# Moving elementwise work between engines in a gated linear attention with a rational MLP: denominator sums, decay products and transposed copies

## The chip, the cores and the metric

One core of a Trainium2 chip. Its engines work side by side, each through its own program in order, and meet at semaphores: TensorE (PE in the profile; its weight loads are PEld), VectorE (DVE), ScalarE (ACT), GpSimd (POOL) and SyncE (SP, which here only issues DMAs). The metric is device time of one execution in microseconds (us); lower is better.

## The reference, cut to what matters

An attention with a per-channel forget gate, 4 batches, 8 heads, 768 steps, 48 channels per head, and behind it an MLP whose activation is a rational function, on 3072 tokens.

```python
f = 1.0 / (1.0 + np.exp(-f_logit))
for t in range(S):
    state = f[:, :, t, :, None] * state + np.einsum('bhd,bhe->bhde', k[:, :, t], v[:, :, t])
    y[:, :, t] = np.einsum('bhd,bhde->bhe', q[:, :, t], state)
...
h = x @ w_in                      # x: 3072 x 384, w_in: 384 x 2048
P = a[0] + a[1] * h + a[2] * h2 + a[3] * h3
Q = 1.0 + np.abs(b[0]) * np.abs(h) + np.abs(b[1]) * h2
out = (P / (Q + 1e-06)) @ w_out
```

The inputs and the output are float32; the kernel's products run in bf16.

## The kernel before, in words

The work is cut into 12 units of 256 tokens, numbered n: unit n holds chunk n // 4 of batch n % 4, both halves of 128 tokens and all 8 heads. Units of one batch pass a state on, so unit n needs the state that unit n - 4 left.

Each unit goes through some thirty named steps, one small function each. The attention part:

- `ld` (L182) loads f, k, q through SP and v through GpSimd's queue. `ef` (L260) and `ls` (L264) on ScalarE make log(1 + exp(-f)); `cs` (L269) sums it along the steps by a matmul with a triangular matrix; `A` (L280) is its exponential with the sign for q (x = 0) or k (x = 1).
- `xa` (L288, the multiplication is L291) multiplies q or k by that decay: 128 partitions x 768, float32 in, bf16 out to `qkp`. Unit 0 does this in two halves, the 11 other units whole, so there are 22 whole products and 4 halves.
- `T` (L300) turns q and k over on TensorE; `Te` (L310, L315) copies the result, 128 x 2048 bf16, from PSUM to SBUF.
- `sc` (L319) makes the scores, `mk` (L333, L337) masks them, `sv` (L382) and `st` (L417) carry the state on, `yb`, `yi` (L367, L360) make y. They use `vm` (L339, L344), two small copies of parts of v on GpSimd. `ye` (L403) brings y to SBUF.

The MLP part, in halves of 8 of 16 blocks of the hidden size (a half is 128 x 2048):

- `h` (L423) is x @ w_in for 4 blocks, `hy` (L440) its copy to bf16, `sq` (L444, L446) h squared, `ab` (L452, L454) |h|, as `z`. The coefficients are scaled beforehand so that the denominator needs only the plain sum z + h squared.
- That sum is made in one of three ways. `u` (L457, L462) adds on TensorE: for 4 blocks, two matmuls with the identity for h squared and two for z into the same PSUM tile, which `ln` (L470, L473) on ScalarE then reads, 128 x 1024 at a time. `zd` (L480, L482) adds with a DMA that accumulates into z, and `lz` (L484, L487) takes the logarithm of z, 128 x 2048 at a time. `zv` (L476) adds on VectorE, also ahead of `lz`; nothing calls it in the kernel before. In before, half 0 to 8 of every unit goes through `u`, half 8 to 16 through `zd`.
- `ex` (L490, L495) makes exp(-log), the reciprocal of the denominator. `p1` (L498, L500), `p2` (L503, L505) and `pm` (L512, L514) make the two parts of the numerator on VectorE, `ta` (L516, L518) adds them with an accumulating DMA from GpSimd's queue, and `gm` (L524, L527) multiplies by the reciprocal.
- `o` (L529, L535) is the product with w_out, `oe` (L538) its copy out of PSUM, `so` the store.

PSUM is four slots, each used by one tile at a time: the number behind @ in a step names its slot. The pools of SBUF tiles are small: three buffers for what `ld` fills, three for `hy` and `gall`, two for `h2` and `z`, one for most of the attention.

The order is written out by hand: `manual_schedule` (L146) lets nothing be reordered, and ORDER (L19) is a list of all steps, split at ";". Each step is issued in that order on its engine, so the list sets every engine's program and the order within each DMA queue; waits between engines follow from the tiles. A step reads `name unit arguments`: `xa 1 0` is unit 1's product for q, `h 0 12 16 @0` is unit 0's blocks 12 to 15 into slot 0, `Te 0 0 2` is a half of unit 0's heads.

Of the kernel before, what the change touches and what calls it, by code (L numbers as in the profile page):

```python
# [29 lines left out]
hy 1 4 8; xa 2 1; cs 3 @2; hy 1 0 4; ld 4 k; p2 0 0 16; T 2 @3; A 3 0; u 0 0 4 @1; pm 0 8 16; A 3 1  # L30
u 0 4 8 @0; ld 5 f; ln 0 0 4; pm 0 0 8; ta 0 8 16; h 1 8 12 @2; ln 0 4 8; Te 2; vm 2 0; vm 2 1; lz 0 8 16
ta 0 0 8; ld 4 q; sq 1 0 8; sc 2 0 @0; h 1 12 16 @3; wo 0 4; ef 4; xa 3 1; sv 2 0 @1; hy 1 8 12; mk 2 0
ae 2; hy 1 12 16; xa 3 0; ls 4; sc 2 1 @3; st 2 0; T 3 @2; ex 0 0 8; mk 2 1; vm 3 1; vm 3 0; yb 2 0 2 @0
sq 1 8 16; yb 2 2 4; yi 2 1; sv 2 1; ye 2 s; cs 4 @3; Te 3; h 2 0 4 @0; A 4 0; st 2 1; A 4 1; ab 1 0 8
# [563 lines left out]
```

## Time and profile before

| | us |
|---|---|
| runs shown, median (lowest to highest) | 239.4 (238.78 to 239.57) |
| profiled execution | 240.47 |
| its span, first to last instruction of the program | 238.8 |

| engine | busy us | share of the span | instructions |
|---|---|---|---|
| TensorE | 213.7 | 89% | 3113 |
| VectorE | 206.0 | 86% | 232 |
| ScalarE | 190.6 | 80% | 197 |
| GpSimd | 61.7 | 26% | 91 |

Busy time is the time in which an engine has an instruction at work; matmuls are pipelined and their ends are modelled, so TensorE's figure is not TensorE at its peak. The DMA queues moved 43.71 MB; the queue of GpSimd's own DMAs 24.38 MB of it. The granted TensorE clock was 0.996 on mean.

In a line of the groups stand: the kernel's line, engine, operation, tile written <- tiles read, shapes, number; then busy us and mean ns of one; then the idle time of the engine just before them and what ended it. In a line of the timeline: start, duration, engine, line, operation, and in square brackets the idle time before it. L numbers are lines of the kernel before.

### The profile page before, as it was taken

The page shows a single profiled execution, that of the slowest core. Times are in us where ns is not written, and L with a number is a line of the kernel's source. Part 1 is how long each engine was busy: PE and PEld are TensorE (multiplying, and loading weights), DVE is VectorE, ACT ScalarE, POOL GpSimd, SP SyncE. Part 2 cuts the span into 40 slices and gives each one's busy share as a digit, 9 for nine tenths or more (in the row PEclk, how much of TensorE's full clock was granted, in tenths as well). Part 3 has the DMA queues.
Part 4 walks back from the last instruction along what each step waited for, and adds up shares of the span by engine and source line. Part 5 has one row for each costly group of instructions (what it writes and reads, how often), then busy time and mean ns, then how long its engine had stood idle before and what let it go on. Part 6 is the DMA issues. An engine that isn't in the chain of part 4 may idle for free.

```text
span 238.8 us, 7065 instructions
## 1 busy us (share of the span) xinstructions
PE 213.7 (89%) x3113; PEld 148.6 (62%) x3128; DVE 206.0 (86%) x232; ACT 190.6 (80%) x197; POOL 61.7 (26%) x91
## 2 busy tenths in 40 slices
PE   0489988798999989799999999999999999999990
PEld 0357765576575658467668778556866877764550
DVE  5395799989989699879899999998999899999630
ACT  4451879979969859959989999997966996999951
POOL 5322044231222205142404133304003311323200
PEclk9999999999999999999999999999999999999998
DMA  7999999999799999999895998799907995499954
GB/s 118 249 191 194 223 222 211 238 222 168 137 178 182 240 218 243 226 216 217 198 188 104 224 232 163 136 227 271 185 7 108 191 204 114 88 176 199 176 118 125
DMA packets 62239, 43.71 MB, mean 183 GB/s; under 512 B 51329, under 2 KB 57217, under 8 KB 62209
## 3 DMA queue, kind: packets, MB, share of 16 engines
q0 software_dynamic: 20976, 24.38, 62.6%
q1 hardware_dynamic: 41088, 18.88, 33.2%
q8 instruction: 24, 0.39, 0.6%
q14 instruction: 7, 0.05, 0.1%
q10 hardware_dynamic: 144, 0.00, 0.0%
HBM read 25.17 MB, written 4.72 MB: 125 GB/s over the span
## 4 chain that ended last, share of the span: by engine, by line
PE 63%; ACT 10%; DMA 10%; issue 7%; DVE 4%; SPq 4%; ACTq 0%; DVEq 0%; POOLq 0%
PE hp L428 22%; PE op L535 18%; PE u L462 6%; PE y L351 5%; DMA qn<-in_q_dram 5%; DMA gall<-hy 4%; PE tp L307 4%; SPq L190 3%; PE sc L329 3%; ACT qi L495 2%; PE cs L277 2%; ACT lq L487 2%; PE sv L399 2%; ACT hy L442 2%; ACT lq L473 2%
## 5 line engine op out<-in xcount | busy, mean ns | idle before, releaser
L535 PE MATMUL op<-w_out_sb,gall 128*128 128x384 bf16 x384 | 69.4, 327 | 3.5 <-issue 1.8
L428 PE MATMUL hp<-xT,w_in_sb 128*128 128x256 bf16 x576 | 68.6, 273 | 1.1 <-ACT xT L407 0.9
L428 PEld LDWEIGHTS <-w_in_sb 128*128 128x128 bf16 x576 | 55.2, 98 | 11.4 <-issue 1.3
L442 ACT CAST hy<-hp 128x1024 bf16<-128x1024 f32 x48 | 47.8, 1016 | 10.7 <-PE hp L428 10.4
L535 PEld LDWEIGHTS <-gall 128*128 128x128 bf16 x384 | 35.7, 98 | 28.7 <-issue 3.4
L495 ACT ACTIVATE qi<-lq 128x2048 bf16<-128x2048 f32 x24 | 45.9, 1918 | 0.2
L518 POOL DMA_DIRECT2D gall<-hy x24 | 22.4, 962 | 71.5 <-DVE gall L514 19.7
L527 DVE TENSOR_TENSOR gall<-gall,qi 128x2048 bf16<-128x2048 bf16 x24 | 29.2, 1219 | 4.0 <-DMA gall<-hy 2.4
L337 DVE TENSOR_TENSOR scm<-sc,mask 128x1024 bf16<-128x1024 f32 x24 | 29.0, 1219 | 3.2 <-PE sc L329 3.0
L482 POOL DMA_DIRECT2D z<-h x12 | 12.8, 1070 | 70.4 <-DVE z L454 22.4
L446 DVE TENSOR_TENSOR h<-hy 128x2048 bf16<-128x2048 bf16 x24 | 29.1, 1218 | 1.2 <-ACT hy L442 1.2
L514 DVE TENSOR_TENSOR gall<-gall,h 128x2048 bf16<-128x2048 bf16 x24 | 28.9, 1217 | 0.0
L473 ACT ACTIVATE lq<-u 128x1024 f32<-128x1024 f32 x24 | 24.2, 1031 | 3.1 <-PE u L462 2.7
L286 ACT ACTIVATE A<-cs 128x768 f32<-128x768 f32 (+1 forms) x26 | 18.7, 767 | 5.9 <-PE cs L277 5.5
L487 ACT ACTIVATE lq<-z 128x2048 f32<-128x2048 bf16 x12 | 23.0, 1921 | 0.0
L315 DVE COPY qkT<-tp 128x2048 bf16<-128x2048 bf16 (+1 forms) x13 | 14.8, 1139 | 5.5 <-PE y L351 3.2
L407 ACT ACTIVATE xT<-y 128x768 bf16<-128x768 f32 x12 | 9.7, 812 | 9.6 <-PE y L351 9.6
L277 PE MATMUL cs<-lsp,Ui 128*128 128x384 bf16 (+1 forms) x39 | 11.0, 347 | 7.2 <-ACT lsp L267 7.2
L454 DVE TENSOR_SCALAR z<-hy 128x2048 uint16<-128x2048 uint16 x24 | 16.8, 711 | 0.0
L344 POOL COPY vmp<-vn 128x128 bf16<-128x128 bf16 x24 | 11.8, 572 | 19.3 <-DMA vn<-in_v_dram 19.3
L505 DVE TENSOR_SCALAR hy<-hy,a_sb 128x4096 bf16<-128x4096 bf16 x12 | 16.6, 1384 | 0.0
L307 PE MATMUL tp<-ident,qkp 128*128 128x128 bf16 x192 | 14.8, 235 | 2.0 <-DVE qkp L291 1.9
(63 smaller groups left out, 269.4 us busy)
## 6 DMA issues: line engine op xcount, KB each, us to landing
gall<-hy POOLq DMA_DIRECT2D x24, 512.0 KB, 7.2
z<-h POOLq DMA_DIRECT2D x12, 512.0 KB, 6.1
out_dram<-osb SPq DMA_DIRECT2D x24, 192.0 KB, 3.9
fn<-in_f_logit_dram SPq DMA_DIRECT2D x11, 384.0 KB, 10.2
kn<-in_k_dram SPq DMA_DIRECT2D x11, 384.0 KB, 7.5
qn<-in_q_dram SPq DMA_DIRECT2D x11, 384.0 KB, 9.4
vn<-in_v_dram POOLq DMA_DIRECT2D x12, 192.0 KB, 8.8
w_out_sb<-in_moe_w_out_dram POOLq DMA_DIRECT2D x4, 384.0 KB, 9.7
```

The costliest lines, as they stand in the source:

```text
L307: nc.tensor.transpose(t[:, x, i, p, :], s["qk"][:, x, i, 2 * p:2 * p + 2, :].rearrange("t h d -> t (h d)"), ident)
L337: return nc.vector.tensor_mul(t, s["sc", g].rearrange("s r a i t -> s (r a) (i t)"), mb)
L428: nc.tensor.matmul(t[:, m - m0, :].rearrange("f (j t) -> f j t", j=UB), w_in_sb[:, kk, m * P:(m + 1) * P], s["x"][:, :, kk, :], start=(kk ...
L442: nc.scalar.copy(fl(big(s, "hy", "hy", 3), m0, m1), fl(s["hp", m0], 0, m1 - m0))
L446: return nc.vector.tensor_mul(fl(big(s, "h2", "h2", 2), m0, m1), fl(s["hy"], m0, m1), fl(s["hy"], m0, m1))
L473: nc.scalar.activation(fl(lq(s, g), m0 - 8 * g, m1 - 8 * g), fl(s["u", m0], 0, m1 - m0), AF.Ln, scale=regs[2], bias=1.0 + 1e-6)
L487: nc.scalar.activation(fl(lq(s, g), m0 - 8 * g, m1 - 8 * g), fl(s["z"], m0, m1), AF.Ln, scale=regs[2], bias=1.0 + 1e-6)
L495: nc.scalar.activation(fl(s["qi", g], m0 - 8 * g, m1 - 8 * g), fl(s["lq", g], m0 - 8 * g, m1 - 8 * g), AF.Exp, scale=-1.0)
L514: return nc.vector.tensor_mul(fl(s["g"], m0, m1), fl(s["g"], m0, m1), fl(s["h2"], m0, m1))
L518: nc.gpsimd.dma_start(out=fl(s["g"], m0, m1), in_=fl(s["hy"], m0, m1), accum_op=ALU.add)
L527: return nc.vector.tensor_mul(fl(s["g"], m0, m1), fl(s["g"], m0, m1), fl(s["qi", g], m0 - 8 * g, m1 - 8 * g))
L535: nc.tensor.matmul(s["op"][:, j, 0:DM], s["g"][:, m, C * j:C * j + C], w_out_sb[:, m, :], start=(s["on", j] == 1), stop=(s["on", j] == KF))
```

## The change

1. 20 of the 24 `u` steps with their 20 `ln` go (those of unit 1 and unit 11 stay). The 10 halves without them go through `zv` on VectorE or `zd` by DMA, and then `lz`. There are 12 `zd` before and after, of which 6 are the same halves; 6 others go from `zd` to `zv`, and 6 new ones come to `zd`. `zv` then does 10 halves: 0 (both), 2 (both), 1, 5, 6, 8 (8 to 16), 3, 4 (0 to 8).
2. 15 of the 22 whole products `xa` get a `p` and run on GpSimd, in its queue between DMA issues and `vm` copies.
3. `Te` of units 1, 2, 4, 10 and 11 get an `s` and run on ScalarE.
4. ORDER is another one throughout: 804 steps in place of 824. The loads at the start change places too.

The function `xa`, whose other form of the option goes:

```diff
-    def xa(n, x, a0=0, a1=HP, eng="v", mark=None):
+    def xa(n, x, *args):
         s = unit(n)
+        a0, a1 = [v for v in args if v != "p"] or (0, HP)
         hh = slice(2 * a0, 2 * a1)
-        i = (nc.gpsimd if eng == "p" else nc.vector).tensor_mul(
+        return (nc.gpsimd if "p" in args else nc.vector).tensor_mul(
             s["qk"][:, x, :, hh, 0:D],
             s["qk"[x]][:, hh].rearrange("p h i d -> p i h d"),
             s["A", x].rearrange("p i (h d) -> p i h d", h=H)[:, :, hh])
-        if mark is not None:
-            behind(i, mark)
-        return i
```

ORDER's start, before and after:

```diff
-cz 0; ab_ b a; ld 0 f 2 4; ld 0 v; ld 0 f 0 2; cz 3; cu 1; ld 0 k 0 2; cz 1; cu 0; ld 0 q 2 4; fa
-ld 0 q 0 2; ef 0 2 4; ld 0 k 2 4; cz 2; ef 0 0 2; ls 0 0 2; fr; ls 0 2 4; ci; cs 0 2 4 @1; vm 0 1
-ld 1 f; cs 0 0 2 @0; A 0 1 0 2; A 0 1 2 4; xa 0 1 0 2; A 0 0 2 4; vm 0 0; wi 8 16; ld 1 v; A 0 0 0 2; wi 4 8; xa 0 0 2 4
-ld 1 k; xa 0 0 0 2; xa 0 1 2 4; T 0 0 2 @2; T 0 2 4 @1; Te 0 0 2; Te 0 2 4; sc 0 0 @2; ld 1 q; sv 0 0 @0
...
-yb 0 0 2 @1; ld 2 f; yi 0 1; xa 1 0; yb 0 2 4; ld 2 q; wi 0 4; ye 0 s; fb; T 1 @3; st 0 1; h 0 12 16 @0
-Te 1; ld 3 f; sc 1 0 @2; hy 0 12 16; h 0 8 12 @1; mk 1 0; ef 2; vm 1 0; vm 1 1; sc 1 1 @3; ls 2; ld 2 v
...
+ci; ld 0 k 0 2; cu 0; ld 0 f 0 2; ab_ b a; ld 0 f 2 4; ld 0 v; cz 3; cz 1; cu 1; ld 0 q 2 4; ld 1 f; cz 2; ld 0 k 2 4
+cz 0; ld 0 q 0 2; ef 0 2 4; ld 1 k; fa; ld 1 q; ls 0 2 4; ef 0 0 2; ls 0 0 2; cs 0 2 4 @0; ld 2 f; cs 0 0 2 @3
+A 0 1 0 2; A 0 0 0 2; A 0 1 2 4; xa 0 1 0 2; ef 1; xa 0 1 2 4; ls 1; vm 0 1; wi 8 16; xa 0 0 0 2; cm; ab_ a s; ld 1 v
+sv 0 0 @2; A 0 0 2 4; wi 0 4; T 0 0 2 @3; cs 1 @1; xa 0 0 2 4; A 1 1; ae 0; Te 0 0 2; A 1 0; ld 3 f; T 0 2 4 @3
+xa 1 1; xa 1 0 p; sc 0 0 @1; Te 0 2 4; st 0 0; sc 0 1 @0; yi 0 1 @3; mk 0 0; vm 0 0; fr; mk 0 1; ef 2; T 1 @1; ld 2 q
+fb; yb 0 0 2; ls 2; Te 1 s; sv 0 1; wi 4 8; yb 0 2 4; st 0 1; sc 1 1 @0; ld 2 k; ld 3 q; mk 1 1; ye 0 s; ld 2 v
+cs 2 @1; sc 1 0 @3; A 2 1; A 2 0; ld 3 k; vm 1 0; mk 1 0; h 0 12 16 @2; ef 3; xa 2 0; h 0 8 12 @0; hy 0 12 16
+hy 0 8 12; sq 0 8 16; vm 1 1; sv 1 0 @3; h 0 0 4 @0; ld 3 v; ls 3; ld 4 f; ld 4 k; wo 8 12; ae 1; st 1 0; ab 0 8 16
```

A stretch of the middle, around unit 6's products, before (the lines of ORDER from `cs 6` on) and after:

```diff
-hy 4 12 16; ld 8 f; gm 2 0 8; ld 6 v; cs 6 @3; hy 4 0 4; pm 3 8 16; sc 5 0 @0; h 4 4 8 @1; ld 9 f; A 6 0
-mk 5 0; vm 5 0; vm 5 1; A 6 1; o 2 0 0 4 @2; ef 7; pm 3 0 8; sv 5 0 @3; hy 4 4 8; ld 7 k; o 2 1 0 4; xa 6 1
-o 2 0 4 8; ae 5; ls 7; st 5 0; yb 5 0 2 @0; ex 3 0 8; xa 6 0; yb 5 2 4; yi 5 1; o 2 1 12 16; p2 3 0 16
-T 6 @1; lz 3 8 16; ab 4 0 8; yi 5 0; ta 3 0 8; o 2 1 8 12; Te 6; sv 5 1; ta 3 8 16; o 2 1 4 8; ye 5 s
...
+o 1 1 0 4; cs 6 @2; zd 3 8 16; o 1 0 8 12; A 6 0; sv 4 1; gm 2 0 8; A 6 1; h 4 8 12 @0; so 0 0 2 s; oe 1 0 2 s
+h 4 12 16 @2; sc 5 1 @3; hy 4 8 12; hy 4 12 16; pm 3 8 16; so 1 0 2 s; st 4 1; h 4 4 8 @0; lz 3 0 8; mk 5 1; xa 6 0 p
+h 4 0 4 @2; o 2 1 4 8 @1; ld 9 f; hy 4 4 8; sv 5 0 @3; sq 4 8 16; ab 4 8 16; hy 4 0 4; o 2 0 0 4; ab 4 0 8; ls 7
+sq 4 0 8; o 2 0 12 16; zd 4 8 16; lz 3 8 16; ae 5; sc 5 0 @0; p2 3 0 16; ex 3 8 16; yi 5 0 @2; o 2 1 8 12; pm 3 0 8
+o 2 0 4 8; yb 5 2 4; ld 10 f; o 2 1 0 4; o 2 1 12 16; st 5 0; ex 3 0 8; mk 5 0; sv 5 1; yi 5 1; ta 3 8 16; st 5 1
+vm 6 1; xa 6 1 p; zv 4 0 8; ta 3 0 8; p1 4 0 16; yb 5 0 2; ld 7 v; cs 7 @0; ye 5 s; o 2 0 8 12; T 6 @3; A 7 0; ld 8 q
+sv 6 0 @2; A 7 1; Te 6; ef 8; h 5 4 8 @0; oe 2 0 2 s; ae 6; so 2 0 2 s; pm 4 8 16; hy 5 4 8; p2 4 0 16; xa 7 0 p
+ld 9 k; ls 8; h 5 0 4 @1; hy 5 0 4; sc 6 0 @3; cs 8 @0; mk 6 0; xa 7 1 p; st 6 0; ld 11 f; pm 4 0 8; gm 3 8 16
```

More of the change, by code (lines that the diff above doesn't have):

```diff
@@ L30 @@
[L30 to L34, printed above, removed]
@@ new lines @@
+p2 5 0 16; ye 7 s; pm 5 8 16; sv 7 1; ef 11; o 4 0 4 8; st 7 1; T 8 @1; ta 5 0 8; ta 5 8 16; ld 10 v; vm 9 0
+o 4 1 0 4; oe 4 0 2 s; zv 6 8 16; p1 6 0 16; h 7 12 16 @3; sv 8 0 @2; Te 8; cs 9 @0; so 4 0 2 s; hy 7 12 16; pm 6 0 8
+ae 8; vm 8 1; h 7 8 12 @3; lz 6 0 8; hy 7 8 12; h 7 0 4 @1; st 8 0; A 9 1; h 7 4 8 @2; p2 6 0 16; gm 5 0 8; ab 7 8 16
+A 9 0; hy 7 0 4; sq 7 8 16; o 5 1 0 4 @0; pm 6 8 16; sc 8 1 @1; hy 7 4 8; zd 7 8 16; xa 9 0; ta 6 0 8; gm 5 8 16
+mk 8 1; sc 8 0 @3; ls 10; o 5 0 0 4; o 5 1 4 8; cs 10 @2; o 5 0 12 16; ex 6 0 8; xa 9 1 p; lz 6 8 16; vm 8 0; A 10 0
@@ new lines @@
+sc 9 0 @2; sc 9 1 @0; yi 9 0 @1; sq 8 0 8; yi 9 1; o 6 0 8 12; mk 9 1; o 6 1 12 16; ex 7 0 8; o 6 0 12 16; o 6 1 8 12
+o 6 1 0 4; mk 9 0; ta 7 0 8; yb 9 0 2; oe 6 0 2 s; p1 8 0 16; yb 9 2 4; ab 8 0 8; zd 8 0 8; ye 9 s; T 10 @0; Te 10 s
+zv 8 8 16; h 9 4 8 @3; hy 9 4 8; h 9 0 4 @2; pm 8 0 8; sc 10 1 @3; so 6 0 2 s; p2 8 0 16; hy 9 0 4; ta 8 0 8
+lz 8 8 16; h 9 12 16 @0; pm 8 8 16; h 9 8 12 @1; gm 7 8 16; hy 9 12 16; sq 9 0 8; sv 10 0 @2; hy 9 8 12; ab 9 0 8
+o 7 1 8 12 @0; ex 8 8 16; gm 7 0 8; zd 9 0 8; sq 9 8 16; ab 9 8 16; o 7 0 8 12; sc 10 0 @1; o 7 0 4 8; o 7 1 4 8
@@ new lines @@
+o 7 1 0 4; vm 11 0; lz 8 0 8; o 7 1 12 16; o 7 0 12 16; ae 10; ex 8 0 8; mk 10 1; xa 11 0 p; o 7 0 0 4; mk 10 0
+zd 9 8 16; p1 9 0 16; T 11 @3; st 10 0; yi 10 0 @1; oe 7 0 2 s; vm 11 1; yi 10 1; vm 10 0; yb 10 0 2; yb 10 2 4
+p2 9 0 16; pm 9 8 16; Te 11 s; ye 10 s; gm 8 0 8; sv 11 0 @0; sc 11 0 @2; lz 9 0 8; h 10 4 8 @1; h 10 12 16 @3
+mk 11 0; ae 11; hy 10 4 8; st 11 0; h 10 8 12 @1; hy 10 12 16; pm 9 0 8; ta 8 8 16; ta 9 8 16; gm 8 8 16; sc 11 1 @0
+h 10 0 4 @2; hy 10 8 12; yb 11 0 2 @3; mk 11 1; yi 11 0; lz 9 8 16; ab 10 8 16; sq 10 8 16; ta 9 0 8; yb 11 2 4
@@ new lines @@
+pm 11 0 8; p2 11 0 16; u 11 0 4 @2; o 9 0 4 8; gm 10 8 16; ta 11 0 8; o 9 0 12 16; ln 11 4 8; ln 11 0 4; pm 11 8 16
+o 9 0 8 12; gm 10 0 8; o 10 0 8 12 @0; ta 11 8 16; o 10 1 12 16; lz 11 8 16; o 10 0 12 16; o 10 1 8 12; o 10 0 4 8
+o 10 0 0 4; o 10 1 0 4; ex 11 0 8; oe 8 0 2 s; o 10 1 4 8; gm 11 0 8; so 8 0 2 s; o 11 0 4 8 @2; ex 11 8 16
+o 11 1 4 8; o 11 0 0 4; o 11 1 0 4; oe 9 0 2 s; gm 11 8 16; oe 10 0 2 s; so 9 0 2 s; o 11 0 8 12; o 11 1 12 16
+so 10 0 2 s; o 11 1 8 12; o 11 0 12 16; oe 11 0 2 s; so 11 0 2 s
```

100 lines of the change are left out of this document (35 added, 65 removed).

## The prediction

> **What bounds the kernel now.** I read the page's busy times first, then a table of three stretches, then the groups by shape, then the timeline where GpSimd and VectorE meet.
>
> ```profile
> PE 213.7 (89%) x3113; PEld 148.6 (62%) x3128; DVE 206.0 (86%) x232; ACT 190.6 (80%) x197; POOL 61.7 (26%) x91
> ...
> PE   0489988798999989799999999999999999999990
> ...
> DVE  5395799989989699879899999998999899999630
> ```
>
> TensorE and VectorE are full in the same slices: neither alone is the bound. The table by stretch (time, busy PE, PEld, DVE, ACT, POOL) says how full.
>
> ```profile
> 0.00:30.00 30.00, 19.74 (x330) 14.20 (x331) 18.88 (x47) 14.49 (x22) 8.32 (x22) 1.00 1.11 195
> 30.00:220.00 190.00, 181.26 (x2711) 127.18 (x2724) 180.25 (x181) 164.93 (x167) 51.69 (x67) 1.00 0.97 185
> 220.00:238.80 18.80, 12.69 (x77) 7.19 (x75) 6.82 (x6) 11.13 (x9) 1.69 (x2) 0.95 0.65 142
> ```
>
> In the 190 us of the middle TensorE idles 8.7, VectorE 9.75, ScalarE 25.1. So taking work from TensorE gains only as much as VectorE can follow; VectorE decides the sum. The middle is where nearly all of the change lies.
>
> **The change, part by part.** The rows that price it, by shape (busy us, mean ns):
>
> ```profile
> L442 ACT CAST hy<-hp 128x1024 bf16<-128x1024 f32 x48 | 47.8, 1016 | 10.7 <-PE hp L428 10.4
> L446 DVE TENSOR_TENSOR h<-hy 128x2048 bf16<-128x2048 bf16 x24 | 29.1, 1218 | 1.2 <-ACT hy L442 1.2
> L473 ACT ACTIVATE lq<-u 128x1024 f32<-128x1024 f32 x24 | 24.2, 1031 | 3.1 <-PE u L462 2.7
> L487 ACT ACTIVATE lq<-z 128x2048 f32<-128x2048 bf16 x12 | 23.0, 1921 | 0.0
> L315 DVE COPY qkT<-tp 128x2048 bf16<-128x2048 bf16 x11 | 13.4, 1221 | 5.1 <-PE y L351 3.2 <-PE tp L307 1.8
> L291 DVE TENSOR_TENSOR qkp<-kn,A 128x768 bf16<-128x768 f32 x11 | 10.5, 951 | 2.1 <-DMA kn<-in_k_dram 1.8 <-ACT A L286 0.3
> ```
>
> TensorE: 20 of 24 u steps go, 4 matmuls each. The chain of work has four of them in 0.86 us at 144.75 us, so 20 × 0.86 = 17.2 us go. It had 8.7 idle in the middle; it will have some 25.
>
> VectorE, work alone: its instructions overlap by some 85 ns, so one costs its distance to the next in the timeline: 0.87 us for a product (L291), 1.13 for a 2048-column copy or tensor operation. 15 products go, -13.0; 5 transposed copies (L315) go, -5.65; 10 sums z + h (zv) come, priced as L446, which has the same shape and kinds, +11.3. Sum **-7.4**.
>
> ScalarE: 5 copies of 128x2048 from PSUM, which no row shows. L442 takes 1016 for 1024 columns and L407 812 for 768, 0.8 ns a column, so 1.83 us, 9.2 in all; 20 ln of 1.03 become 10 lz of 1.92, -1.4. Sum +7.8, covered by its 25.1 idle us in the middle; without that cover it would cost these 7.8. I take 0.
>
> DMAs: 12 accumulating zd remain 12 and 24 ta remain 24, of 512 KB each; the loads are the same. Only other halves go by DMA. Bytes cost 0; the new places of the loads are in the term for the start.
>
> GpSimd: 15 products of 128x768, two inputs. No row shows one. The nearest is L344, a copy of 128 columns with one input, 0.29 us when nothing is in its way. Six times its columns is 1.75 us; twice that, for two inputs, 3.5; VectorE's 0.95 is the lower end. I take 1.75, since the copy's time holds a fixed part that is not paid six times. The Trainium skill, GPSIMD Engine Reference, 3.1 Elementwise, gives about 2.6 cycles an element for two inputs at 1.2 GHz, an estimate of 1.7 us here; no run here shows it.
>
> What such a product does to VectorE is the dearest unknown. This is the timeline of both engines where copies meet them (start, duration, x2 is two merged):
>
> ```profile
> 105.14 2.35 DVE L446 TENSOR_TENSOR h<-hy 128x2048 bf16<-128x2048 bf16 x2
> 107.41 1.34 DVE L500 TENSOR_SCALAR gall<-hy,a_sb 128x4096 bf16<-128x4096 bf16 x1
> ```
> ```profile
> 107.21 1.67 POOL L344 COPY vmp<-vn 128x128 bf16<-128x128 bf16 x1
> ...
> 186.37 0.30 POOL L344 COPY vmp<-vn 128x128 bf16<-128x128 bf16 x1 [4.40 <-DMA vn<-in_v_dram]
> ```
>
> At 186.37 VectorE multiplies scores out of PSUM (L337) and the copy takes 0.30. At 107.21 VectorE works from SBUF: the copy began 0.28 before L446's end, was not done when L500 took over, and ended 0.13 us after L500. It took 1.67. The other way round is seen with a DMA's issue: L454, 0.69 as a rule, took 1.32 at 31.9, while GpSimd issued one from 31.4 on. So they hold each other up, unless VectorE reads PSUM (L337 29.0, L315 14.8, L419 11.0: 54.8 of 206 us, 27%; about a quarter after the change).
>
> Hence a product takes from VectorE between nothing (it falls beside PSUM work or idle time) and its whole 1.75 us: 0 to 26 for 15. If it meets VectorE at random, three quarters: 1.31. If VectorE's back-to-back instructions keep it out until a PSUM instruction of 1.13 comes, as at 107.2, 0.62. I take the mean, 0.96, so **+14.4**. This is more than the 0.87 that VectorE saved on it.
>
> VectorE's idle 9.75: the waits table puts 3.2 on y before L315, 3.0 on sc before L337, 2.3 on tp before L315, all TensorE, 8.5 in all. A freer TensorE can remove these (0 to -8.5). I take half, **-4.25**: the scores and states still come in a chain through ScalarE and VectorE itself.
>
> New waits: GpSimd's queue is in order, and behind each product stand ta and zd issues, loads of v and vm copies. In before gm (L527) waited 2.4 us in all for ta, so most have slack. The transposes are nearer: xa 6 1 on GpSimd, then T 6, then Te 6 on VectorE, with only zv 4 0 8 and p1 4 (2.4 us) between, against 1.75 + 1.0 of transposes + 0.6 to get in. One such microsecond, **+1** (0 to +5).
>
> Start: the load of q for unit 1 was the start's chain; it stays ninth on SP's queue, issued at 8.95, landed at 19.7. Its product now runs on GpSimd (+0.8) and Te 1 on ScalarE (+0.6), and h 0, at 22.04 in before, now stands behind sc 1 1, cs 2 and sc 1 0 on TensorE: about 26. But mk 1 and xa 2 0 are done by then, which before came later. Also on GpSimd, vm 0 0, w_in's third load and v for unit 2 wait behind that product; on SP, load 1 f (0.93 to issue) goes ahead of two halves of unit 0. I take **+2** (-1 to +4). End: the steps from h 11 on hold the same ScalarE work but one lz for two ln; 0.
>
> Sum: -7.4 + 14.4 - 4.25 + 1 + 2 = +5.75. The profiled execution took 240.47 (span 238.8 and 1.67 around it): 246.2. The median of the runs is 1.07 below it: **245.1 us**.
>
> **The rivals.**
> *Faster: the products fall beside PSUM work.* GpSimd has 177 idle us, TensorE is relieved, and all three engines could run near 198. Then a product takes 0.27 from VectorE (+4), the TensorE waits go wholly: -7.4 + 4 - 8.5 + 0 + 2 = -9.9, less 1.07: 229.5; with half of those waits 233.8; I put it at 232. It decides from 0.58 us a product down: (7.4 + 4.25 - 1 - 2) / 15. For it: at 180 to 187 us most copies met L315 or L337 and were not held. Against: a product is six times as long as a copy.
>
> *Whole exclusion.* The product holds VectorE's SBUF work for all its length whenever it has begun: 15 × 1.31 = 19.7 in place of 14.4, so +11: 250.4. The Trainium skill, SBUF — State Buffer, Who interferes with whom, speaks for it and against this change: a VectorE instruction with two SBUF inputs, or in a two-port mode, and a GpSimd instruction that reads SBUF lock each other out for the whole instruction. By that rule the 1.67 above is explained, and the trace agrees.
>
> *GpSimd's queue becomes the wait.* VectorE's runs keep products out for 2 to 3 us and the ta behind them reach gm late. Were every second product to pass 2.5 us on, 7 × 2.5 = 17: about 260. Against: gm's slack in before.
>
> **How the numbers follow.** Forecast 0.38 (own range 240.2 to 248, from 0.63 to 1.15 a product); faster 0.30; whole exclusion 0.17; queue 0.07; within 0.3% 0.08 (the terms cancel). This kernel's measurement can tell about 0.3% from no change, 238.7 to 240.1. So faster 0.30, same 0.08, slower 0.62. The range 231 to 257 takes in most of the faster case and whole exclusion with some queueing, and leaves out about 0.15.
>
> **What would show it.** Right: VectorE's busy time near 206 or above, with L291 down to 11 and L446, L514, L527, L454 longer than 1.22 and 0.69 on mean (or gaps before them with no releaser); GpSimd products of 1.75 to 4 us; TensorE near 196 with gaps before T and h. Wrong: those VectorE means unchanged, VectorE near 198 and TensorE's gaps small; then the faster case holds. If waits of L527 on ta lead the list, it is the queue. h 0 well before 26 us unmakes the start's term.

## The result, and the profile after

The changed kernel takes **248.68 us** (median of 4 runs, 247.75 to 249.15); the kernel before, run on the same chip, 239.09. The ratio is 1.0406, with a 95% interval of 1.0351 to 1.046. Forecast were 245.1 and the range 231 to 257: the sign and the range held, and the time lies 0.7 us above the forecast's own range. The profiled execution took 249.15 and its span 247.3, that is 8.5 more than before. Of a3, b2 and c1 below some executions were disturbed and took over 1.5% more than the fastest; the medians count these, the ratios leave them out, and the profiles of a3 and c1 are of such executions.

The page's busy times and slices (one digit for 6.2 us here) of the kernel after:

```profile
PE 206.3 (83%) x3045; PEld 146.0 (59%) x3048; DVE 208.6 (84%) x222; ACT 198.0 (80%) x192; POOL 103.9 (42%) x106
...
PE   0576987639958998999879999979979979799990
...
DVE  5373384999999989989999999999999995999630
...
PEclk9999999988995999999979999999999999999998
```

VectorE now leads, and its row is 9 from the eighth slice on almost without a break, while TensorE's has 7s among its 9s. Ahead of the eighth slice VectorE is emptier than before. Three stretches (time, busy PE, PEld, DVE, ACT, POOL, granted clock, DMA share, GB/s):

```profile
0.00:60.00 60.00, 38.90 (x637) 28.37 (x638) 38.91 (x67) 37.29 (x44) 24.59 (x35) 0.97 1.12 210
60.00:220.00 160.00, 146.90 (x2293) 105.75 (x2287) 154.76 (x143) 142.10 (x134) 73.35 (x67) 0.97 0.89 168
220.00:247.30 27.30, 20.47 (x126) 11.88 (x124) 14.96 (x14) 18.63 (x15) 5.96 (x5) 0.97 0.76 157
```

The first two of these stretches before:

```profile
0.00:60.00 60.00, 45.44 (x759) 33.39 (x762) 47.71 (x77) 41.20 (x53) 17.18 (x35) 1.00 1.14 204
60.00:220.00 160.00, 155.56 (x2281) 107.99 (x2293) 151.43 (x151) 138.22 (x137) 42.83 (x54) 1.00 0.94 180
```

VectorE's idle time (the stretch less its busy time) was 12.3, 8.6 and 12.0 us before (the last stretch to 238.8); it is 21.1, 5.2 and 12.3 now. So the 8.5 us of span are 2.6 more work of VectorE (208.6 against 206.0) and 5.9 more idle time: +8.8 at the start, -3.3 in the middle and +0.4 at the end.

The groups by shape:

```profile
L434 DVE TENSOR_TENSOR h<-hy 128x2048 bf16<-128x2048 bf16 x24 | 33.3, 1388 | 1.0 <-ACT hy L430 0.9
L502 DVE TENSOR_TENSOR gall<-gall,h 128x2048 bf16<-128x2048 bf16 x24 | 31.7, 1329 | 0.0
L325 DVE TENSOR_TENSOR scm<-sc,mask 128x1024 bf16<-128x1024 f32 x24 | 28.6, 1213 | 4.6 <-PE sc L317 4.6
L283 POOL TENSOR_TENSOR qkp<-kn,A 128x768 bf16<-128x768 f32 x8 | 22.0, 2753 | 17.0 <-DMA kn<-in_k_dram 12.9 <-ACT qi L483 4.1
L442 DVE TENSOR_SCALAR z<-hy 128x2048 uint16<-128x2048 uint16 x24 | 19.3, 803 | 0.7 <-ACT hy L430 0.7
L493 DVE TENSOR_SCALAR hy<-hy,a_sb 128x4096 bf16<-128x4096 bf16 x12 | 17.8, 1482 | 0.0
L283 POOL TENSOR_TENSOR qkp<-qn,A 128x768 bf16<-128x768 f32 x7 | 16.9, 2408 | 3.3 <-ACT A L277 3.3
L303 ACT COPY qkT<-tp 128x2048 bf16<-128x2048 bf16 x5 | 9.3, 1865 | 1.3 <-PE y L339 1.2
```

Lines are 8 to 12 lower than before: h squared is L434 (was L446), the `pm` product L502 (L514), |h| L442 (L454), `p2` L493 (L505), the product with decay L283 (L291). Before, three of them read:

```profile
L514 DVE TENSOR_TENSOR gall<-gall,h 128x2048 bf16<-128x2048 bf16 x24 | 28.9, 1217 | 0.0
L454 DVE TENSOR_SCALAR z<-hy 128x2048 uint16<-128x2048 uint16 x24 | 16.8, 711 | 0.0
L505 DVE TENSOR_SCALAR hy<-hy,a_sb 128x4096 bf16<-128x4096 bf16 x12 | 16.6, 1384 | 0.0
```

The means of the first four rose from 1218, 1217, 711 and 1384 ns to 1388, 1329, 803 and 1482. That of L325 (was L337), which reads scores from PSUM, did not (1219 to 1213). A product takes 2.4 to 2.8 us on GpSimd on mean.

### The profile page after: what moved, and what is told of

Its sections match the earlier page's. It is cut to its first block, busy times and chain, and to the rows that moved or that the text cites. A ratio compares the mean times of both kernels' runs of the same rounds, so it can differ in the third digit from the quotient of the medians.

```text
span 247.3 us, 6916 instructions
## 1 busy us (share of the span) xinstructions
PE 206.3 (83%) x3045; PEld 146.0 (59%) x3048; DVE 208.6 (84%) x222; ACT 198.0 (80%) x192; POOL 103.9 (42%) x106
## 4 chain that ended last, share of the span: by engine, by line
DVE 39%; PE 20%; DMA 16%; ACT 10%; issue 7%; SPq 4%; POOL 2%; ACTq 0%; DVEq 0%; POOLq 0%
DVE h L434 8%; PE op L523 6%; DMA qn<-in_q_dram 6%; DVE gall L502 6%; DVE scm L325 6%; PE hp L416 5%; DMA fn<-in_f_logit_dram 5%; DVE hy L493 4%; DVE z L442 4%; DVE gall L515 4%; DMA gall<-hy 4%; SPq L181 3%; PE y L339 3%; ACT hy L430 3%; DVE gall L488 3%
## 5 line engine op out<-in xcount | busy, mean ns | idle before, releaser
L416 PEld LDWEIGHTS <-w_in_sb 128*128 128x128 bf16 x576 | 56.6, 100 | 14.3 <-issue 5.0
L475 ACT ACTIVATE lq<-z 128x2048 f32<-128x2048 bf16 x22 | 42.3, 1925 | 0.0
L506 POOL DMA_DIRECT2D gall<-hy x24 | 24.3, 1031 | 42.8 <-DVE gall L502 19.6
L434 DVE TENSOR_TENSOR h<-hy 128x2048 bf16<-128x2048 bf16 x24 | 33.3, 1388 | 1.0 <-ACT hy L430 0.9
L470 POOL DMA_DIRECT2D z<-h x12 | 11.7, 978 | 50.8 <-DVE z L442 18.9
L325 DVE TENSOR_TENSOR scm<-sc,mask 128x1024 bf16<-128x1024 f32 x24 | 28.6, 1213 | 4.6 <-PE sc L317 4.6
L502 DVE TENSOR_TENSOR gall<-gall,h 128x2048 bf16<-128x2048 bf16 x24 | 31.7, 1329 | 0.0
L283 POOL TENSOR_TENSOR qkp<-kn,A 128x768 bf16<-128x768 f32 x8 | 22.0, 2753 | 17.0 <-DMA kn<-in_k_dram 12.9
L332 POOL COPY vmp<-vn 128x128 bf16<-128x128 bf16 x24 | 19.0, 812 | 13.7 <-DMA vn<-in_v_dram 13.7
L442 DVE TENSOR_SCALAR z<-hy 128x2048 uint16<-128x2048 uint16 x24 | 19.3, 803 | 0.7 <-ACT hy L430 0.7
L253 ACT ACTIVATE fn<-fn 128x768 f32<-128x768 f32 (+1 forms) x13 | 10.3, 795 | 11.8 <-DMA fn<-in_f_logit_dram 11.7
L283 POOL TENSOR_TENSOR qkp<-qn,A 128x768 bf16<-128x768 f32 x7 | 16.9, 2408 | 3.3 <-ACT A L277 3.3
L493 DVE TENSOR_SCALAR hy<-hy,a_sb 128x4096 bf16<-128x4096 bf16 x12 | 17.8, 1482 | 0.0
L488 DVE TENSOR_SCALAR gall<-hy,a_sb 128x4096 bf16<-128x4096 bf16 x12 | 16.4, 1368 | 0.0
```

What stands on the lines that cost most here:

```text
L283: return (nc.gpsimd if "p" in args else nc.vector).tensor_mul(s["qk"][:, x, :, hh, 0:D], s["qk"[x]][:, hh].rearrange("p h i d -> p i h d") ...
L325: return nc.vector.tensor_mul(t, s["sc", g].rearrange("s r a i t -> s (r a) (i t)"), mb)
L416: nc.tensor.matmul(t[:, m - m0, :].rearrange("f (j t) -> f j t", j=UB), w_in_sb[:, kk, m * P:(m + 1) * P], s["x"][:, :, kk, :], start=(kk ...
L434: return nc.vector.tensor_mul(fl(big(s, "h2", "h2", 2), m0, m1), fl(s["hy"], m0, m1), fl(s["hy"], m0, m1))
L442: return nc.vector.tensor_scalar(fl(big(s, "z", "z", 2), m0, m1).bitcast(U16), fl(s["hy"], m0, m1).bitcast(U16), 0x7FFF, None, op0=ALU.bit ...
L475: nc.scalar.activation(fl(lq(s, g), m0 - 8 * g, m1 - 8 * g), fl(s["z"], m0, m1), AF.Ln, scale=regs[2], bias=1.0 + 1e-6)
```

## The experiments

The theory from these rows: VectorE is the bound; it got ten sums that TensorE and the DMAs had done, and what the products and the copies took from it came back as longer instructions and waits. The rivals: the new order's start costs the time; or the products do, by exclusion; or the copies are not free on ScalarE; or the sums would have been free elsewhere. The kernels undo one part in the new order (a), add one part alone to the kernel before, in its order (b), or move the sums (f, c). "Work" below is VectorE's busy time, "idle" the span less that.

### Products and start in the new order

**a1_products_back**: the 15 products return to VectorE, at their places.

```diff
-xa 1 1; xa 1 0 p; sc 0 0 @1; Te 0 2 4; st 0 0; sc 0 1 @0; yi 0 1 @3; mk 0 0; vm 0 0; fr; mk 0 1; ef 2; T 1 @1; ld 2 q
+xa 1 1; xa 1 0; sc 0 0 @1; Te 0 2 4; st 0 0; sc 0 1 @0; yi 0 1 @3; mk 0 0; vm 0 0; fr; mk 0 1; ef 2; T 1 @1; ld 2 q
...
```

> The changed kernel with its 15 products back on VectorE, each at its place in the new order; nothing else differs. Port theory (the products on GpSimd hold VectorE's work on SBUF up for about as long as they save): VectorE gets 15 x 0.87 = 13 us of work and loses the some 10 us by which its instructions were lengthened in the changed kernel, so its busy time goes from 208.6 to about 212 and the time stays within 3 us of 248.7; were the exclusion the cause of the whole loss, it would come down to 242 or less. Start theory (the first 60 us of the new order are late, and that is the loss): the first h still ends at about 27 us and the time stays at 247 to 252. The lengthened rows (h<-hy 1388 ns, gall<-gall,h 1329) go back to about 1.22 us by either.

Measured 244.39 us, ratio 1.0248 (1.0168 to 1.0328), between what the two theories expected: the products on GpSimd cost about 4 us in this order (4.3 by the medians), and without them it is still slower than before. Its groups, and two of its stretches of 20 us:

```profile
L434 DVE TENSOR_TENSOR h<-hy 128x2048 bf16<-128x2048 bf16 x24 | 29.2, 1216 | 0.0
L502 DVE TENSOR_TENSOR gall<-gall,h 128x2048 bf16<-128x2048 bf16 x24 | 29.0, 1215 | 0.0
```
```profile
60.00:80.00 20.00, 18.13 (x271) 13.20 (x271) 20.00 (x21) 18.07 (x19) 9.33 (x6) 1.00 1.02 190
...
180.00:200.00 20.00, 17.79 (x342) 13.43 (x327) 20.00 (x20) 17.87 (x16) 7.42 (x9) 0.97 0.90 177
```

The VectorE instructions are short again, so the products had made them long. VectorE is busy 20.00 of 20 us in each of the seven stretches from 60 to 200, with TensorE at 17.6 to 18.8 and ScalarE at 17.6 to 19.0: here it alone is the bound. Its work is 209.6, 1.0 more than after, though it does 15 products (13.0 us) more: lengthening had eaten some 12 of the 13. From the means, after less a1: L434 24 × 0.172 = 4.1, L502 24 × 0.114 = 2.7, L442 24 × 0.111 = 2.7, L493 12 × 0.145 = 1.7, together 11.3 or 0.75 a product (GpSimd's own DMA issues are the same in both). The two spans differ by 4.4 us: after has 1.0 less work and 5.4 more idle time.

Of these 5.4, 1.7 lie before 60 us, 3.6 between 60 and 220, and 0.1 behind. The largest single piece of the middle is one wait of 2.2 us, which ends at 209.09 when the `ta` for `gm` 8 8 16 lands. In the chain that ended last, after's way to it leads over a product in GpSimd's queue:

```profile
196.34 0.14 POOL qkp L283
196.49 1.60 issue
198.09 1.76 POOL z L470
199.85 0.24 POOL vmp L332
200.09 8.97 DMA gall<-hy
```

GpSimd issued this `ta` 10.25 us after the `ta` before it (189.84, 200.09); in a1 it was 8.46 (185.46, 193.92). The difference, 1.8 us, is the length of the product that stands between them (1.82), and in a1 no `gm` of the middle waits for a `ta`. So this part is the queue's rival come true, on a small scale. The other waits were not traced to their products.

What a product meets shows in the timeline of after, VectorE first, then GpSimd:

```profile
44.48 1.22 DVE L466 TENSOR_TENSOR z<-z,h 128x2048 bf16<-128x2048 bf16 x1
45.61 2.35 DVE L502 TENSOR_TENSOR gall<-gall,h 128x2048 bf16<-128x2048 bf16 x2
47.88 2.84 DVE L493 TENSOR_SCALAR hy<-hy,a_sb 128x4096 bf16<-128x4096 bf16 x1
...
136.02 1.22 DVE L303 COPY qkT<-tp 128x2048 bf16<-128x2048 bf16 x1
137.16 0.55 DVE L407 TENSOR_TENSOR state<-sv,alast 128x384 bf16<-128x384 f32 x1
138.19 2.35 DVE L325 TENSOR_TENSOR scm<-sc,mask 128x1024 bf16<-128x1024 f32 x2 [0.48 <-PE sc L317]
```
```profile
44.60 5.04 POOL L283 TENSOR_TENSOR qkp<-kn,A 128x768 bf16<-128x768 f32 x1 [12.90 <-DMA kn<-in_k_dram]
...
136.22 1.97 POOL L283 TENSOR_TENSOR qkp<-kn,A 128x768 bf16<-128x768 f32 x1
138.26 1.94 POOL L283 TENSOR_TENSOR qkp<-qn,A 128x768 bf16<-128x768 f32 x1
```

At 136 to 140 VectorE reads PSUM: both products take under 2 us and nothing of VectorE's is longer. At 44.60 VectorE works from SBUF: the product is held through L466 and both L502, which follow one another without a gap (it ends 1.68 us after them, about its own 1.81), and L493 is held by it (2.84 in place of 1.34). Both engines lose. The rule of the Trainium skill that the prediction weighed (SBUF — State Buffer, Who interferes with whom: the shared ports are locked for a whole instruction, by whichever issued first) has the trace on its side, with one thing more: here a run of three VectorE instructions kept the product out past the first one's end.

**a2_start_order**: after, with the start's order mended (seven steps move). ScalarE no longer meets unit 2's `ef` ahead of unit 1's copy, nor TensorE unit 2's `cs` ahead of the first `h`.

```diff
-fb; yb 0 0 2; ls 2; Te 1 s; sv 0 1; wi 4 8; yb 0 2 4; st 0 1; sc 1 1 @0; ld 2 k; ld 3 q; mk 1 1; ye 0 s; ld 2 v
-cs 2 @1; sc 1 0 @3; A 2 1; A 2 0; ld 3 k; vm 1 0; mk 1 0; h 0 12 16 @2; ef 3; xa 2 0; h 0 8 12 @0; hy 0 12 16
...
+fb; yb 0 0 2; Te 1 s; sv 0 1; wi 4 8; yb 0 2 4; st 0 1; sc 1 1 @0; ld 2 k; ld 3 q; mk 1 1; ye 0 s; ef 2; ls 2; ld 2 v
+sc 1 0 @3; ld 3 k; vm 1 0; mk 1 0; h 0 12 16 @2; h 0 8 12 @0; cs 2 @1; hy 0 12 16
...
```

> The changed kernel with nine steps of its start moved behind unit 0's first h: ef 2, ls 2, cs 2, A 2, xa 2 0 and ef 3, so that ScalarE does not stand before the load of f for unit 2 (landed at 21.3 us) while unit 1's copy of transposes and unit 0's y wait in its queue. Start theory: the first h ends at 22 to 24 us in place of 27.7, and 3 to 5 us of that reach the end: 244 to 246. Port theory, and also if the loads of unit 2 and 3 are the start's limit further on: the first h comes earlier, but the second half of unit 0 and unit 1 are as late as before, and the time stays at 247 to 249.

The reason is in after's timeline of ScalarE and VectorE at the start:

```profile
21.28 0.84 ACT L253 ACTIVATE fn<-fn 128x768 f32<-128x768 f32 x1 [5.47 <-DMA fn<-in_f_logit_dram]
22.90 1.85 ACT L303 COPY qkT<-tp 128x2048 bf16<-128x2048 bf16 x1
```
```profile
31.64 0.96 DVE L283 TENSOR_TENSOR qkp<-qn,A 128x768 bf16<-128x768 f32 x1 [2.95 <-DMA qn<-in_q_dram]
...
40.61 0.96 DVE L283 TENSOR_TENSOR qkp<-qn,A 128x768 bf16<-128x768 f32 x1 [3.18 <-DMA qn<-in_q_dram]
```

ScalarE stood 5.47 us for unit 2's f, with unit 1's transposed copy queued behind it. VectorE then stood for the q of units 2 and 3. Measured 247.67 us, ratio 1.0378 (1.0314 to 1.0442), 1.0 less than after: less than the intervals can part. Unit 0's first h squared started at 27.5 in place of 32.7, but its second half's at 40.4 in place of 41.5, right behind the q product of unit 3 in both: the wait for that load gave the start's gain back.

**a3_start_and_product**: a2, and unit 3's q product moved behind the work that waited for nothing, for the second load. **a4_start_products_back**: a3 with the products on VectorE.

```diff
-yb 1 2 4 @3; vm 2 1; xa 3 0; hy 0 4 8; yi 1 1; sq 0 0 8; yb 1 0 2; lz 0 8 16; ab 0 0 8; ye 1 s; p1 0 0 16; Te 2 s
-h 1 0 4 @0; zv 0 0 8; h 1 4 8 @3; hy 1 0 4; ef 4; pm 0 0 8; ld 6 f; sv 2 0 @1; pm 0 8 16; hy 1 4 8; p2 0 0 16
+yb 1 2 4 @3; vm 2 1; hy 0 4 8; yi 1 1; sq 0 0 8; yb 1 0 2; lz 0 8 16; ab 0 0 8; ye 1 s; p1 0 0 16; Te 2 s
+h 1 0 4 @0; zv 0 0 8; h 1 4 8 @3; hy 1 0 4; ef 4; pm 0 0 8; ld 6 f; sv 2 0 @1; pm 0 8 16; xa 3 0; hy 1 4 8; p2 0 0 16
```

> The start's order of a2, and the product of q for unit 3, for whose load VectorE stood still for 3.2 us at 39.5 us, moved behind unit 0's pm; products on GpSimd as in the changed kernel. Start theory: what a2 gained at the first h (4 us) was lost again to three loads that VectorE waits for in its order (30, 34 and 39 us); without the last of them 2 to 4 us more come through, 244 to 246 us. If the start is made up for later anyway (VectorE catches up beside TensorE): 247 to 248.

> As a3, and the 15 products on VectorE. If start and products are two losses that add: a3 less the 4.3 us that a1 gained, so 240 to 242. If VectorE's work is what is left (209.6 us in a1, 3.6 more than before), it stays 2 to 4 us above the kernel before, 241 to 243.

a3: 245.52 us, ratio 1.0187 (1.0094 to 1.0281). a4: 243.01, 1.0172 (1.0115 to 1.0228); its ratio is below a1's, but their intervals overlap. Those of a3 and a4 cover each other, so the pair does not price the products again. a4's middle:

```profile
60.00:220.00 160.00, 148.22 (x2307) 106.50 (x2305) 158.12 (x158) 145.25 (x135) 58.11 (x56) 0.98 0.91 173
```

VectorE idles 1.9 us of 160. An order can gain hardly more there; only less work for VectorE can.

### Each part alone, in the order of before

**b1_products_only**, **b2_sums_only**, **b3_copies_only**, **b4_copies_and_sums** (b2 and b3 together):

```diff
-yb 0 0 2 @1; ld 2 f; yi 0 1; xa 1 0; yb 0 2 4; ld 2 q; wi 0 4; ye 0 s; fb; T 1 @3; st 0 1; h 0 12 16 @0
+yb 0 0 2 @1; ld 2 f; yi 0 1; xa 1 0 0 4 p; yb 0 2 4; ld 2 q; wi 0 4; ye 0 s; fb; T 1 @3; st 0 1; h 0 12 16 @0
...
```
```diff
-u 4 4 8 @0; hy 5 0 4; h 5 12 16 @3; gm 3 8 16; ls 8; o 3 0 0 4 @1; ae 6; ln 4 4 8; xa 7 1; ld 11 f
+zv 4 0 8; hy 5 0 4; h 5 12 16 @3; gm 3 8 16; ls 8; o 3 0 0 4 @1; ae 6; lz 4 0 8; xa 7 1; ld 11 f
...
```
```diff
-Te 1; ld 3 f; sc 1 0 @2; hy 0 12 16; h 0 8 12 @1; mk 1 0; ef 2; vm 1 0; vm 1 1; sc 1 1 @3; ls 2; ld 2 v
+Te 1 s; ld 3 f; sc 1 0 @2; hy 0 12 16; h 0 8 12 @1; mk 1 0; ef 2; vm 1 0; vm 1 1; sc 1 1 @3; ls 2; ld 2 v
...
```

b1 moves the change's 15 products; b2 turns the `u` and `ln` pairs of units 0 and 2 to 10 into ten `zv` and `lz`; b3 moves the change's five copies.

> The kernel before, in its own order, with the same 15 products on GpSimd; nothing else. Port theory: VectorE saves 13 us of work and is held up for 10 to 14, the GpSimd queue adds a little: 237 to 243, no gain worth the name. If the products fall beside PSUM work: VectorE is 13 us freer, but TensorE stays full (181 of 190 us in the middle), so 235 to 238. If the queue of GpSimd's DMAs is the wait: over 245, with gm waiting for ta.

> The kernel before, in its own order, with the 20 u and ln steps of units 0 and 2 to 10 replaced by 10 zv on VectorE and 10 lz on ScalarE at the same places; the zd stay where they were. TensorE loses 17 us of work, VectorE gets 11.3. If VectorE is as much the bound as TensorE (my reading): 11.3 more on VectorE, of which at most its 8.5 us of waits for TensorE are given back, so 241 to 247, slower. If TensorE alone bounds: 228 to 235, faster.

> The kernel before with the copies of transposes of units 1, 2, 4, 10 and 11 on ScalarE; nothing else. VectorE has 5.65 us less work, ScalarE 9.2 more, of its 25 idle in the middle. If VectorE bounds beside TensorE: 235 to 238. If TensorE holds the time by itself or ScalarE's longer chain delays the scores: 238 to 241.

> The kernel before with the 10 sums on VectorE (b2) and the 5 copies on ScalarE; products on VectorE, the old order. This is the changed kernel's division of work without its products and its order; a1 is the same division in the new order (other halves by DMA): 244.4. If time follows VectorE's work: b2's 248.1 less 5.65, 242 to 243.5, so the new order would cost 1 to 2 us. If the new order is worth something by itself: b4 above 245.

Products alone 244.17 us, ratio 1.0238 (1.0167 to 1.0309); sums alone 248.11, 1.0372 (1.0289 to 1.0454); copies alone 241.94, 1.0151 (1.0076 to 1.0225); copies and sums 249.94, 1.0461 (1.0403 to 1.0519). Each part costs by itself: no interval takes in 1, though that of copies alone allows less than 1%. The busy times of b1, b2's middle, and b3's longest wait of VectorE (us, times, longest):

```profile
PE 215.0 (89%) x3128; PEld 148.7 (62%) x3128; DVE 210.8 (87%) x217; ACT 190.7 (79%) x197; POOL 95.5 (40%) x106
...
L446 DVE TENSOR_TENSOR h<-hy 128x2048 bf16<-128x2048 bf16 x24 | 34.3, 1437 | 0.8 <-ACT hy L442 0.8
```
```profile
30.00:220.00 190.00, 165.43 (x2610) 120.08 (x2608) 182.87 (x183) 158.39 (x152) 54.37 (x65) 0.96 0.93 177
```
```profile
DVE scm L337 <- PE sc L329: 11.7, 8, 2.8
```

b1: VectorE lost 13.0 us of products and has 4.8 more work than before: 17.8 of lengthening, 1.19 a product (24 × 0.22 on L446, 24 × 0.24 on L527, the rest on five smaller groups). b2: TensorE idles 24.6 of 190 us (8.7 before) and VectorE 7.1 (9.75 before): 16 us of TensorE bought 2.6 of VectorE's idle time, and VectorE had 10.1 more to do. b3: VectorE's work fell by 5.6, as it should, but it now waits 11.7 us for scores, 3.0 before. In part the copy brings them later: unit 11's starts at 194.82 in place of 193.87, behind an `ex` in ScalarE's queue, and its scores at 199.44 in place of 198.22. In part VectorE, with less to do, only comes to wait earlier: the scores of unit 10 start at 185.02 in place of 185.18, and VectorE waits 2.3 us for them in place of 0.65. In the new order the wait for scores is 3.9 (a1), so there the copies seem covered; no run takes them back in that order.

b4 divides the work as a1 does, in the old order and with other halves by DMA. Its ratio is 1.0461 against a1's 1.0248, and it idles 3.6 us more (the table below): for all that its start loses, the new order with its choice of halves is worth some 5 us. That does not make up for the work that came to VectorE.

### The sums elsewhere

**b5_sums_by_dma**: before, the `u` of units 2 to 10 replaced by `zd` (21 `zd` in place of 12). **f1_new_order_dma_sums**: a4, seven of the ten `zv` replaced by `zd`.

```diff
-hy 3 4 8; ex 1 8 16; p1 2 0 16; o 0 0 8 12; o 1 0 0 4 @1; ab 2 0 8; o 1 0 4 8; oe 0 0 2 s; gm 1 8 16
+hy 3 4 8; ex 1 8 16; p1 2 0 16; o 0 0 8 12; o 1 0 0 4 @1; ab 2 0 8; zd 2 0 8; o 1 0 4 8; oe 0 0 2 s; gm 1 8 16
...
```
```diff
-o 0 0 8 12; ex 1 0 8; st 3 0; mk 3 0; zv 2 0 8; pm 1 8 16; sv 3 1; cs 5 @1; A 5 0; zv 2 8 16; o 0 1 8 12; o 0 1 12 16
+o 0 0 8 12; ex 1 0 8; st 3 0; mk 3 0; zd 2 0 8; pm 1 8 16; sv 3 1; cs 5 @1; A 5 0; zd 2 8 16; o 0 1 8 12; o 0 1 12 16
...
```

> The kernel before, old order, products and copies on VectorE; the u and ln steps of units 2 to 10 give way to zd, an accumulating DMA issued as soon as z and h squared of that half are there, with lz right ahead of ex. TensorE loses 15.5 us, VectorE's work stays at 206, the DMAs move 9 x 512 KB more. If VectorE is the bound and TensorE only rides beside it: 236 to 239.5, little or nothing. If TensorE bounds: 228 to 232. If the 9 accumulating DMAs are in the way of the others: over 242, with gm or lz waiting for them.

> a4 (the changed kernel with the start moved and the products back on VectorE) with 7 of its 10 sums on VectorE (units 2 to 6 and 8) made by accumulating DMAs instead, lz of unit 8 put right ahead of its ex. VectorE's work goes from 209.9 to 202. If time follows VectorE's work and the new order's waits stay small: 243 less 7.9, 234 to 237, faster than the kernel before. If the DMAs' landing (some 6 us) takes the place of the work: 239 to 243.

b5: 263.83 us, ratio 1.1074 (1.103 to 1.1117). f1: 254.2, 1.064 (1.0583 to 1.0698). The waits that lead: VectorE's in b5, then ScalarE's and VectorE's in f1:

```profile
DVE qkp L291 <- DMA qn<-in_q_dram: 14.0, 4, 10.2
DVE qkp L291 <- DMA kn<-in_k_dram: 6.8, 1, 6.8
```
```profile
ACT lq L475 <- DMA z<-h: 11.2, 3, 8.4
...
DVE h L434 <- ACT hy L430: 15.0, 3, 8.5
```

In b5 VectorE's work is as before (206.6) and TensorE is relieved, yet it is 25 us slower, because VectorE waits for q and k: their loads land 12.2 and 11.1 us after issue, 9.4 and 7.5 before. In f1 ScalarE waits for the sums themselves, and VectorE for ScalarE. As placed here, the DMAs were no free place.

**c1_sums_back** and **c2_half_the_sums_back**: a4 with all ten, or five, of the `zv` turned back into `u` and `ln`, put where I found a PSUM slot free.

```diff
-h 4 12 16 @2; sc 5 1 @3; hy 4 8 12; hy 4 12 16; pm 3 8 16; so 1 0 2 s; st 4 1; h 4 4 8 @0; lz 3 0 8; mk 5 1; xa 6 0
+h 4 12 16 @2; sc 5 1 @3; hy 4 8 12; hy 4 12 16; u 3 0 4 @2; pm 3 8 16; so 1 0 2 s; st 4 1; u 3 4 8 @1; h 4 4 8 @0; ln 3 0 4; ln 3 4 8; mk 5 1; xa 6 0
...
```

> a4 (new order with the start moved, products on VectorE, 5 copies on ScalarE) with all 10 sums back on TensorE: u and ln in place of zv and lz, put where a PSUM slot is free near the place of lz. VectorE's work goes from 209.9 to 198.6, TensorE's up by 17. If time follows VectorE's work: 243 less 11.3, 231 to 236, faster than the kernel before. If TensorE, full again, or ScalarE behind it takes over: 237 to 243.

> a4 with 5 of the 10 sums back on TensorE (0 and 3 and 4, half 0 to 8; 6 and 8, half 8 to 16). VectorE's work goes from 209.9 to 204, TensorE's up by 8.6. If time follows VectorE's work: 236 to 238. If the sums' place in the order matters more than who makes them: 240 to 243.

c1: 266.71 us, ratio 1.1153 (1.1105 to 1.1202). c2: 256.53, 1.0724 (1.0676 to 1.0773). ScalarE's leading wait in c1:

```profile
ACT lq L461 <- PE u L450: 26.5, 14, 4.4
```

ScalarE waits for `u` (2.7 us before), and what stands behind it waits too. I read this as a bad placing, with the sum too close ahead of its reader. VectorE's work fell to 201.6 and 205.6, so the kernels do not show the worth of sums on TensorE. Whether a planned placing would gain in the new order stays open.

### Side by side

Against the profiled execution of before (span 238.8, VectorE's work 206.0, idle 32.8). It took 240.47 us, above the four runs of before at the result (237.73 to 239.57), so the spans here look smaller than the ratios. a3 and c1 have no row, for the reason given there.

| kernel | span | work | idle |
|---|---|---|---|
| after | +8.5 | +2.6 | +5.9 |
| a1, products back | +4.1 | +3.6 | +0.5 |
| a2, start order | +6.5 | +3.0 | +3.5 |
| a4, start and products back | +3.0 | +3.9 | -0.9 |
| b1, products only | +2.8 | +4.8 | -2.0 |
| b2, sums only | +7.5 | +10.1 | -2.6 |
| b3, copies only | +1.2 | -5.6 | +6.8 |
| b4, copies and sums | +10.3 | +6.2 | +4.1 |
| b5, sums by DMA | +23.2 | +0.6 | +22.6 |
| f1, new order, sums by DMA | +14.3 | -3.1 | +17.4 |
| c2, half the sums back | +15.9 | -0.4 | +16.3 |

No kernel tried beats the one before. Six missed their expectation upwards: b1, b2 and b3 by about 1 us, f1, c1 and c2 by 11 us or more.

## Why the prediction was right, and where not

**The bound: right.** "VectorE decides the sum" is what a1 and b2 show: a1's 4.1 us of span are 3.6 of VectorE's work, and taking 80 matmuls from TensorE bought nothing by itself. It holds only where VectorE's waits stay small: b3, f1 and c2 have less of its work than before and are slower.

**TensorE, -17.2: the matmuls went, the time did not.** Busy time fell from 213.7 to 206.3, not to 196. No cost of this shows, since TensorE was not the bound; see the last section.

**VectorE's own work, -7.4: right within 2 us.** b2 gives +10.1 for the sums (forecast +11.3), b3 -5.6 for the copies (-5.65), a1 +3.6 for both (+5.65).

**ScalarE, cost 0: wrong in the old order, not tested in the new.** The copy took 1.865 us (1.83). In the old order moving the copies cost 1.5%; the cover that I named, ScalarE's idle time, is not what matters for a copy that scores wait for.

**The product on GpSimd, 1.75 us: right.** Those that met nothing took 1.81 (the estimate from the Trainium skill, GPSIMD Engine Reference, 3.1 Elementwise, was 1.7), the first number of min/median/max ns in after's rows of that line:

```profile
L283 POOL TENSOR_TENSOR qkp<-kn,A x8: 1807/2612/5044, 44.6 to 174.7; 128x768 bf16<-128x768 f32 x8
L283 POOL TENSOR_TENSOR qkp<-qn,A x7: 1810/1942/4190, 15.9 to 196.3; 128x768 bf16<-128x768 f32 x7
```

**0.96 a product from VectorE: the mechanism right, the size between.** 0.75 in after and 1.19 in b1, so 11.3 and 17.8 in place of 14.4. By the timelines, which VectorE instruction a product falls beside decides. The conclusion that it takes more than the 0.87 it saves holds for b1; in after it takes a little less, and the idle time that goes with the products (+5.4 in after against a1) makes the loss. The term for new waits was forecast as +1, and its path through the transposes is not the one that leads: the `ta` behind a product is (2.2 us).

**VectorE's waits for TensorE, -4.25: right, in part by luck.** The 8.5 us that it halves are rows for the whole span; 6.7 of them lie in the 190 us of the middle, and 5.9 from 60 to 220 us (`y` 2.6, `tp` 1.8, `sc` 1.5). There they fell to 1.5 in after, so by 4.4, and to 1.0 in a1: three quarters of a smaller sum went, not half of 8.5. VectorE's idle time in the stretch fell by 6.9 in a1 and only by 3.3 in after, where new waits came, the 2.2 for a `ta` first.

**Start, +2: this is the step that failed.** Idle time to 60 us rose from 12.3 to 21.1. It is 19.4 in a1, so some 7 of the 8.8 us have nothing to do with the products. I let the load of q for unit 1 set the start and thought that it lands at 19.7 as before; it was in by 15.9, when its product ran. The first `h` started at 27.3 us, near the 26 that I forecast, but by another road: the wait was for f of unit 2, and after it for q of units 2 and 3. The term held the first load and not those behind it, in an order in which all loads moved. The list of VectorE's waits to 60 us bears this out: 10.4 us for loads in place of 3.2 (q 6.1 of them, the coefficients 3.4, k 0.9) and 3.5 for scores in place of 1.5. Mending two of these places (a4) still leaves 17.65: as the waits for q went, others came, for ScalarE's `hy` and for k. How little the best order of the start would leave stays open.

**End, 0: right** (12.0 to 12.3).

So the mechanism of the products was right, but the sum came near in part by luck, by two errors that partly cancel: VectorE's work was forecast at +7.0 (-7.4 + 14.4) and is +2.6; its idle time was forecast at -1.25 (-4.25 + 1 + 2) and is +5.9.

**The rivals.** *Faster*: refuted; the SBUF means rose, and where TensorE's waits did go (a1), VectorE's added work filled the time. *Whole exclusion*: 250.4 is nearer to the result than my 245.1, but its price of 1.31 a product is not found; b1's 1.19 comes near it in the old order. *GpSimd's queue*: `gm` waited 3.6 us for `ta`, 2.4 before and not at all in a1; it does not lead the list, of which q's loads are first with 6.1, but it is the largest wait that the products brought to the middle.

## What to carry to other kernels

Find the engine that is full in each stretch and count its work first: ten sums moved onto it added 10.1 us of work and 7.5 of span in b2, though TensorE was relieved of 16. Then ask whether its waits stay: less work for VectorE gained nothing in b3, f1 and c2, as the waits grew by more. A product on GpSimd is not a free product where VectorE works from SBUF: price it by the timeline of a smaller one, and look at what stands behind it in GpSimd's queue. After a new order, follow every load of the start to its reader, not only the one that was last before.

## What the hardware showed that was not expected

**The granted clock was lower in kernels that leave TensorE more gaps.** Its mean was 0.981 to 0.998 in the runs of before, 0.986 to 0.999 in those of b1 and b3, where TensorE is 89% busy as before, and 0.947 to 0.982 in those of after, b2 and b4, where it does 80 matmuls fewer and is 82 or 83% busy. The number of matmuls alone does not explain it: c1 does them all again, is 83% busy and had 0.954 to 0.973. In after the clock was lowest where TensorE was emptiest in the middle:

```profile
60.00:80.00 20.00, 16.39 (x165) 10.17 (x158) 20.00 (x17) 15.60 (x16) 8.29 (x9) 0.87 0.93 163
```

The busy share of a stretch alone does not set it: 120 to 140 us, with 18.0 busy, had 0.91, and 160 to 180, with 17.6, had 1.00. Of 17.2 us of matmuls taken away, 9.8 did not show in the busy time: the rows of `h`, `o` and `cs` are 1.2, 1.1 and 2.2 us busier, and the rest I have not placed. The Trainium skill, TensorE: Matmul & The Clock Gate, Part 1: The HAM clock gate (the "warmup" mystery), says that the clock is granted by recent activity; these rows agree in the main. It cost nothing that these runs can show, as VectorE was the bound.

**More accumulating DMAs inside SBUF landed later, and some loads with them.** With nine more of 512 KB, q's loads took 12.2 us from issue to landing in place of 9.4, k's 11.1 in place of 7.5 and the sums themselves 7.3 in place of 6.1, and the kernel 10.7% longer (b5). With seven more in the new order (f1 against a4) the sums took 7.8 in place of 4.8 and k's loads 11.8 in place of 10.2, but q's 10.0 in place of 12.5: not every load is slowed.
